# Keys of two token blocks by pairs of tiles, seven products in place of eight

## The chip, the cores and the metric

The kernel runs on one core of a Trainium2 chip. The metric is the device time of one execution in microseconds (us). All data are float32; TensorE gets every operand as two parts, a high part (the value rounded by a copy on ScalarE) and a low part (the rest, a subtraction on VectorE), and each product is three matmuls: high by high, high by low, low by high.

## The reference, cut to what matters

```python
# attention branch, S = 2048 tokens, D = 512, 32 heads of 16
q, k, v = split(x @ wqkv)
phi = lambda t: where(t > 0, t + 1, exp(t)) + 1e-6
kv  = einsum("bhsd,bhse->bhde", phi(k), v);  z = sum over tokens of phi(k)
o   = phi(q) kv / (phi(q) z + 1e-6);         a = o @ wo
# expert branch: 8 experts, softmax of x @ w_gate over all of them
b   = sum over e of gate_e * (silu(x @ w1[e]) @ w2[e])
out = g * a + (1 - g) * b,   g = sigmoid(x . gate_w)
```

The change is in one stage only, called keys: `phi(x @ wk)` for all tokens, ten more columns of the same product (eight gate logits, `x . gate_w` and a zero column), and y = sum over tokens of x^T phi(k), from which kv is made later.

## The kernel before, in words

The program has two stages, `keys` and `experts`, and every engine works through its instructions in the order in which the program issues them (the schedule is written by hand). The keys stage ends after some 96 us; the experts fill the rest. The 2048 tokens are four blocks of 512 (`tb` 0 to 3), each of four tiles of 128 tokens; the 512 features are four slices of 128 (`k`).

For one tile, `g_proj` (L482) makes two groups of the key columns, 256 and 266 wide (the second with the ten extra columns): for each of the four slices three matmuls (L454), 24 in all. `g_done` (L457) evicts a group: `phi_first` (L73) is an exponential and a relu on ScalarE (L74, L75), `phi_last` (L77) joins them on VectorE (L78). After the second group `eps_high` (L84, a ScalarE copy) and `eps_low` (L87, VectorE L88) make the high and low part `pkh` of the keys, VectorE copies the ten extra columns to `lg` (L470), and the keys are added to `pks`, their sum over tokens, by a DMA of GpSimd's queue that accumulates (L473 to L480; from the fifth tile on two tiles are added on VectorE first, L479). `split_xt` (L428) makes high and low part of the tile's tokens in row form, and `y_acc` (L489) adds x^T phi(k) into four PSUM banks `ys` with twelve matmuls 512 wide (L60 to L62). The loop over tiles (L558) issues both groups of tile t, then `split_xt(t)`, then `y_acc(t-1)`, then a list of further work (`beside`): splits of later token blocks (`split_x`), and what the experts need of the tokens.

The experts multiply in pairs of blocks with seven products in place of eight (Strassen-Winograd). For that the first stage makes sums of token blocks: `x_sum` (L498, four VectorE subtractions 1024 wide for each half of the tokens) and `x_part` (L504), which splits a sum into high and low part (one ScalarE copy and one VectorE subtraction, 1024 wide). The first half's seven operands stay in `XO[0]`; the second half's go to a DRAM room `xstash` (`x_keep`, and DMAs in `x_part`, L515) and come back later. `m.prep` (L190) prepares the first expert operands; `touch` (L649) opens the experts on TensorE.

PSUM has eight banks: two with tag "a", one "b", one "c", four "dn" (the four `ys`). Loads are issued on SyncE's queue: `load_x` (L381, a block of tokens by features, 1 MB), `load_xt` (L424, the block by rows, 1 MB). Tiles with one tag share a fixed number of rooms; a new tile waits until the last reader of the room's old one is through.

Of the kernel before, what the change touches and what calls it, by code (L numbers as in the profile page):

```python
# [16 lines left out]
P = 128  # L17
S = 2048
D = 512
# [304 lines left out]
def keys(m):  # L324
# [4 lines left out]

    banks_of = [0]  # L330
# [16 lines left out]
    def x_tiles(tb, K):  # L347
        if (tb, K) in ((0, 0), (0, 1), (1, 1)):
            X[tb, K] = [m.x_tile(f"x{tb}{K}{c}") for c in "hl"]
        elif (tb, K) == (3, 1):  # L350
            X[tb, K] = [m.x_tile(f"x{tb}{K}{c}", "xs") for c in "hl"]
        else:
            X[tb, K] = [att.tile([P, 2, TB], F32R, name=f"x{tb}{K}{c}", tag="xe", bufs=6) for c in "hl"]
# [18 lines left out]

    def room(name, dt=F32):
        return att.tile([P, 2048], dt, name=name, tag="raw", bufs=4)
# [11 lines left out]
    def split_x(tb, k):  # L386
        if k % 2 == 0:
            x_tiles(tb, k // 2)
        split(raw[tb][:, k, :], xk(0, tb, k), xk(1, tb, k))
# [5 lines left out]
    gw = [att.tile([P, 2 * KT * w], F32R, name=f"g{i}") for i, w in enumerate((256, 320))]  # L395
    gw = [g.rearrange("p (c k f) -> p c k f", c=2, k=KT)[:, :, :, :n] for g, n in zip(gw, G)]
    g0, g1 = gw
    x0 = raw[0] = four(room("x0"))
    r0 = four(m.raw_tile("r0")[:, :KT * G[0]])
    r1 = [hl_tile(f"r1{i}", F32) for i in range(2)]  # L400
# [4 lines left out]
    for k in range(KT):  # L405
        for lo, hi in pieces(k):
            nc.sync.dma_start(x0[:, k, lo:hi], m.xT[0][:, k * TB + lo:k * TB + hi])
        for w in ((0,), (1, 2), (3,), ())[k]:
            queue = nc.scalar if w < 2 else nc.sync
            queue.dma_start(r0[:, w, :], m.wk[:, w * G[0]:(w + 1) * G[0]])  # L410
    for i in range(2):
        at = KT * G[0] + 2 * i * G[1]
        nc.sync.dma_start(r1[i][:, :, :G[1]], m.wk[:, at:at + 2 * G[1]].rearrange("p (k f) -> p k f", k=2))
    x_tiles(0, 0), x_tiles(0, 1)
    for k in range(KT):
        for lo, hi in pieces(k):
            act_copy(xk(0, 0, k, lo, hi), x0[:, k, lo:hi])
        split(r0[:, k, :], g0[:, 0, k, :], g0[:, 1, k, :], v.tensor_copy if k == 0 else act_copy)
        v.tensor_sub(xk(1, 0, k), x0[:, k, :], f32(xk(0, 0, k)))
# [8 lines left out]
    def split_xt(t):  # L428
        if t < 12:
            xt[t] = m.w1p.tile([P, 2, TB], F32R, name=f"xt{t}", tag="o", bufs=4)  # L430
        else:
            xt[t] = att.tile([P, 2, TB], F32R, name=f"xt{t}", tag="xe", bufs=6)
# [12 lines left out]
    def bands(t):  # L445
        if t == 5:
            band(mask.rearrange("p (b e) -> p b e", e=DH), [[-DH, P // DH], [0, DH]], 1)

    pk, pk_last = {}, [None]
# [7 lines left out]
    def g_done(t, g, ps):  # L457
        if g == 0:
            if t < NTT:
                h = att.tile([P, 2, TB], F32R, name=f"pkh{t}", tag="xe", bufs=6)  # L460
            else:
                h = hl_tile(f"pkh{t}")
            pk[t] = pks_room if t == 0 else sf_tile(f"pk{t}"), h
            m.phi(pk[t][0][:, :G[0]], ps)
        else:
            d, h = pk[t]
            m.phi(d[:, G[0]:], ps[:, :D - G[0]])
            m.eps_high(h[:, 0], d)
            m.eps_low(h[:, 1], d, h[:, 0])
            v.tensor_copy(lg[:, t, :E + 2], ps[:, D - G[0]:])  # L470

            if t == 0:
                nc.gpsimd.dma_start(pks, d)  # L473
            elif t < NTT:
                nc.gpsimd.dma_start(pks, d, accum_op=ALU.add)
            elif t % 2 == 0:
                pk_last[0] = d
            else:
                v.tensor_add(d, d, pk_last[0])  # L479
# [24 lines left out]
    def x_part(p, i):  # L504
# [16 lines left out]

    idle = dn_bank("idle")
    for i in range(7):
        nc.tensor.matmul(idle, zero[:, :P], zero, start=True, stop=True)
    banks = [up_bank(f"g0_{t}")[:, :G[0]] for t in range(NTT)]
    for k in range(KT):
        for j in range(3):
            for t in range(NTT):
                g_pass(t, 0, k, j, banks[t])
    load_xt(0)  # L530
    load_x(1)
    for k in range(KT):
        split(r1[k // 2][:, k % 2, :G[1]], g1[:, 0, k, :], g1[:, 1, k, :])
    for t in range(NTT):
        g_done(t, 0, banks[t])
    for t in range(NTT):
        split_xt(t)
        g_proj(t, 1, dn_bank if t < 2 else up_bank)
    ys = [dn_bank(f"y{i}") for i in range(KT)]
    load_xt(1)  # L540
    load_x(2)
# [776 lines left out]
```

## Time and profile before

| | us |
|---|---|
| median of 3 runs (2317.18 to 2318.82) | 2317.56 |
| the profiled execution | 2317.11 |
| its span in the profile | 2315.4 |
| TensorE busy | 2309.3 |
| VectorE busy | 1829.0 |
| ScalarE busy | 1407.1 |
| keys: first matmul of the last `y_acc` | 92.85 |
| experts: first matmul (`touch`) | 95.59 |

The span is taken from the first to the last record; the execution's own time lies 1.7 us above it. A row of the timeline gives start, duration, engine, line, operation, output and input. Durations of matmuls are modelled and overlap: the distance from one start to the next is what a matmul costs on TensorE. On ScalarE and VectorE the next queued operation starts some 0.1 us before the recorded end of the one ahead of it.

### The profile page before, as it was taken

The numbers are of one execution on the slowest core, as the hardware profiler recorded it, in microseconds if no ns is written. First come the engines' busy times: TensorE is split into PE (matmuls) and PEld (weight loads), VectorE is DVE, ScalarE is ACT, GpSimd is POOL, SyncE is SP. The second block draws the span as 40 slices with busy tenths as digits, with TensorE's granted clock in tenths as the row PEclk, the third lists the DMA queues.
The fourth block names the chain that finished last, engine by engine and source line by source line (L and its number), as shares of the span: only waits on it lengthen the run. The fifth ranks groups of instructions, "written<-read, shape, count | busy, mean of one in ns | idle before, by whom it ended". The sixth has DMA issues, their size and how long they took to land.

```text
span 2315.4 us, 31620 instructions
## 1 busy us (share of the span) xinstructions
PE 2309.3 (100%) x10546; PEld 1917.3 (83%) x10546; DVE 1829.0 (79%) x3136; ACT 1407.1 (61%) x2654; POOL 156.8 (7%) x216
## 2 busy tenths in 40 slices
PE   9999999999999999999999999999999999999999
PEld 8888888888888888888888888888888888888887
DVE  7899888888888888888677768776677777877777
ACT  6687666666666666666555556555565655655553
POOL 1101000000000000000001000000011101000001
PEclk9999999999999999999999999999999999999999
DMA  6799888988889898888856455664556746566568
GB/s 224 222 306 294 269 277 257 286 258 266 268 270 280 253 293 254 264 269 259 297 146 168 151 179 151 185 186 137 161 175 183 189 147 182 164 164 175 162 219 226
DMA packets 323044, 510.29 MB, mean 220 GB/s; under 512 B 52080, under 2 KB 220416, under 8 KB 322496
## 3 DMA queue, kind: packets, MB, share of 16 engines
q1 hardware_dynamic: 294256, 462.53, 61.2%
q0 software_dynamic: 22912, 44.68, 11.2%
q10 hardware_dynamic: 5712, 1.05, 0.2%
q8 instruction: 83, 1.36, 0.2%
q14 instruction: 81, 0.66, 0.1%
HBM read 342.41 MB, written 163.13 MB: 218 GB/s over the span
## 4 chain that ended last, share of the span: by engine, by line
PE 100%; DVE 0%; issue 0%
PE p L60 16%; PE p L62 16%; PE p L61 16%; PE a L60 9%; PE a L61 9%; PE a L62 9%; PE c L60 5%; PE c L62 5%; PE c L61 5%; PE b L60 2%; PE b L62 2%; PE b L61 2%; PE g L454 2%; PE y L60 1%; PE y L62 1%; PE y L61 1%
## 5 line engine op out<-in xcount | busy, mean ns | idle before, releaser
L62 PE MATMUL p<-ho,w 128*128 128x512 f32 x1602 | 623.3, 389 | 0.0
L60 PE MATMUL p<-ho,w 128*128 128x512 f32 x1602 | 623.2, 389 | 0.0
L61 PE MATMUL p<-ho,w 128*128 128x512 f32 x1602 | 623.2, 389 | 0.0
L790 DVE TENSOR_TENSOR ho<-s,ho 128x512 fp32r<-128x512 f32 x784 | 536.2, 685 | 38.9 <-ACT ho L65 36.3
L65 ACT ACTIVATE ho<-s 128x512 fp32r<-128x512 f32 x784 | 481.5, 621 | 17.4 <-PE p L62 11.0
L60 PEld LDWEIGHTS p<-ho,w 128*128 128x128 f32 x1602 | 300.8, 188 | 62.5
L61 PEld LDWEIGHTS p<-ho,w 128*128 128x128 f32 x1602 | 300.8, 188 | 62.3
L62 PEld LDWEIGHTS p<-ho,w 128*128 128x128 f32 x1602 | 300.6, 188 | 62.4
L65 ACT ACTIVATE o<-rs 128x512 fp32r<-128x512 f32 x224 | 129.1, 576 | 203.6 <-PE c L62 114.1
L65 ACT ACTIVATE o<-rm 128x512 fp32r<-128x512 f32 x240 | 138.4, 577 | 142.4 <-PE a L62 65.6
L716 DVE TENSOR_TENSOR s<-c,s 128x512 f32<-128x512 f32 x116 | 80.1, 691 | 156.2 <-PE c L62 148.0
L65 ACT ACTIVATE ws<-rm 128x256 fp32r<-128x256 f32 (+1 forms) x204 | 114.6, 571 | 46.0 <-DMA w2stash<-ws 40.5
L628 ACT ACTIVATE s<-s 128x512 f32<-128x512 f32 x224 | 138.4, 618 | 6.1 <-DVE s L721 3.5
L628 ACT ACTIVATE s<-b 128x512 f32<-128x512 f32 x112 | 67.0, 599 | 103.1 <-PE b L62 98.1
L65 ACT ACTIVATE s<-a 128x512 f32<-128x512 f32 x116 | 69.1, 595 | 91.2 <-PE a L62 91.2
L205 DVE TENSOR_TENSOR o<-rm,o 128x512 fp32r<-128x512 f32 x180 | 123.0, 683 | 1.3 <-ACT o L65 1.2
L721 DVE TENSOR_TENSOR s<-a,s 128x512 f32<-128x512 f32 x116 | 79.7, 687 | 52.1 <-PE a L62 52.0
L205 DVE TENSOR_TENSOR o<-rs,o 128x512 fp32r<-128x512 f32 x168 | 114.1, 679 | 5.1 <-ACT o L65 5.1
L219 DVE TENSOR_TENSOR ws<-rm,ws 128x512 fp32r<-128x512 f32 x155 | 106.1, 684 | 14.3 <-ACT ws L65 12.6
L65 ACT ACTIVATE b<-a 128x512 f32<-128x512 f32 x116 | 67.2, 579 | 61.1 <-PE a L62 61.1
L849 POOL DMA_DIRECT2D acct<-c x30 | 25.8, 869 | 914.6 <-DVE c L843 712.8
L65 ACT ACTIVATE s<-c 128x512 f32<-128x512 f32 x116 | 68.9, 594 | 22.3 <-PE c L62 22.3
(317 smaller groups left out, 4529.8 us busy)
## 6 DMA issues: line engine op xcount, KB each, us to landing
w<-w2stash SPq DMA_DIRECT2D x403, 512.0 KB, 4.1
w2stash<-ws SPq DMA_DIRECT2D x359, 256.0 KB, 4.6
rm<-wm SPq DMA_DIRECT2D x228, 256.0 KB, 5.2
rs<-wm SPq DMA_DIRECT2D x108, 256.0 KB, 4.0
wb<-wgtd SPq DMA_DIRECT2D x16, 512.0 KB, 4.8
acct<-c POOLq DMA_DIRECT2D x30, 256.0 KB, 6.0
acct<-d POOLq DMA_DIRECT2D x30, 256.0 KB, 5.4
acct<-k POOLq DMA_DIRECT2D x30, 256.0 KB, 5.3
```

Source lines behind the costliest of these rows:

```text
L60: nc.tensor.matmul(ps, wh, xh, start=start, stop=False, skip_group_check=True)
L61: nc.tensor.matmul(ps, wh, xl, start=False, stop=False, skip_group_check=True)
L62: nc.tensor.matmul(ps, wlo, xh, start=False, stop=stop, skip_group_check=True)
L65: nc.scalar.activation(dst, src, AF.Copy, scale=scale, bias=bias)
L205: v.tensor_sub(two(o, 1), src, f32(two(o, 0)))
L219: v.tensor_sub(two(w, 1), src, f32(two(w, 0)))
L454: nc.tensor.matmul(ps, xk((0, 0, 1)[j], tb, k, tt * P, (tt + 1) * P), gw[g][:, (0, 1, 0)[j], k, :], start=(k == 0 and j == 0), stop=(k == ...
L628: nc.scalar.activation(dst, src, AF.Silu)
L716: v.tensor_add(sn[g, 2], bank[g, "c"], sn[g, 2])
L721: v.tensor_add(sn[g, 3], bank[g, "a"], sn[g, 3])
L790: v.tensor_sub(h[1], s, f32(h[0]))
L849: nc.gpsimd.dma_start(m.acct[part.h, j, dt], s, accum_op=ALU.add)
```

## The change

The blocks are taken in the order 2, 3, 0, 1 (`ORD`). Blocks 2 and 3 are done tile by tile as before; the group of 266 columns comes first now, the ten extra columns are copied on ScalarE, and none of these eight tiles is added to another on VectorE. For blocks 0 and 1 the tiles j of both blocks are a pair: the two tiles' keys are a 2 by 2 product (two tiles by two halves of the features, two halves of the features by two halves of the key columns), and seven products of six matmuls each make it (`product`, 266 wide for four of them, 256 for three), with the token sums `XO[0]` that the experts use anyway as the stationary operand, and sums of wk's four blocks as the moving one. These sums are new: `w_load` reads a part of wk a second time, `w_sums` makes four sums on VectorE, and `w_part` splits four of them. The seven products run in banks a, b and c, with a copy of bank a to b and two evictions to `s2` and `s3` on ScalarE, and two additions on VectorE, for each pair. `group`, `late` and `flush` put phi and its splits into the queues; `extra` holds the further work of each pair. `y_acc` can be issued in halves. The token sums of the first half must be ready before the pairs, so those of the second half are made during the pairs, and the raw blocks 2 and 3 are loaded a second time for them (`load_x(2)`, `load_x(3)`); the second half's four split sums share one room (`raw["t"]`) from which they are stored. `m.prep(0, 1)` to `(0, 7)` are issued between the last two `y_acc`.

```diff
+    ORD = (2, 3, 0, 1)
+    ND = 2 * NTT
+    W = (G[1], G[0])
+    OFF = (KT * G[0], 0)
+    WS = (320, 256)
...
+        if (tb, K) == (3, 0):
             X[tb, K] = [att.tile([P, 2, TB], F32R, name=f"x{tb}{K}{c}", tag="xe", bufs=6) for c in "hl"]
+        else:
+            X[tb, K] = [m.x_tile(f"x{tb}{K}{c}", "xs" if tb == 3 else "x") for c in "hl"]
...
-        return att.tile([P, 2048], dt, name=name, tag="raw", bufs=4)
+        return att.tile([P, 2048], dt, name=name, tag="raw", bufs=3)
...
+    sums_of = []
+    def pk_tile(t, h):
+        pk[t] = sf_tile(f"pk{t}") if t != ORD[0] * NTT else pks_room, h
+        return pk[t]
+    def pk_done(t, alone):
+        d, h = pk[t]
+        m.eps_high(h[:, 0], d)
+        m.eps_low(h[:, 1], d, h[:, 0])
+        if alone:
+            sums_of.append(t)
+            nc.gpsimd.dma_start(pks, d, **({} if len(sums_of) == 1 else {"accum_op": ALU.add}))
+        elif not m.odd:
+            m.odd = [d]
+        else:
+            v.tensor_add(d, d, m.odd.pop())
+            nc.gpsimd.dma_start(pks, d, accum_op=ALU.add)
+    m.odd = []
+    def group_done(t, g, src):
+        d = pk[t][0]
+        if g == 0:
+            act_copy(lg[:, t, :E + 2], src[:, HALF:W[0]])
+        m.phi(d[:, HALF:] if g == 0 else d[:, :HALF], src[:, :HALF])
     def g_pass(t, g, k, j, ps):
@@ -454,44 +491,29 @@
         nc.tensor.matmul(ps, xk((0, 0, 1)[j], tb, k, tt * P, (tt + 1) * P), gw[g][:, (0, 1, 0)[j], k, :],
                          start=(k == 0 and j == 0), stop=(k == KT - 1 and j == 2))
-    def g_done(t, g, ps):
+    def g_done(t, g, ps, alone):
         if g == 0:
-            if t < NTT:
-                h = att.tile([P, 2, TB], F32R, name=f"pkh{t}", tag="xe", bufs=6)
-            else:
-                h = hl_tile(f"pkh{t}")
-            pk[t] = pks_room if t == 0 else sf_tile(f"pk{t}"), h
-            m.phi(pk[t][0][:, :G[0]], ps)
-        else:
-            d, h = pk[t]
-            m.phi(d[:, G[0]:], ps[:, :D - G[0]])
-            m.eps_high(h[:, 0], d)
-            m.eps_low(h[:, 1], d, h[:, 0])
-            v.tensor_copy(lg[:, t, :E + 2], ps[:, D - G[0]:])
-            if t == 0:
-                nc.gpsimd.dma_start(pks, d)
-            elif t < NTT:
-                nc.gpsimd.dma_start(pks, d, accum_op=ALU.add)
-            elif t % 2 == 0:
-                pk_last[0] = d
-            else:
-                v.tensor_add(d, d, pk_last[0])
-                nc.gpsimd.dma_start(pks, d, accum_op=ALU.add)
-    def g_proj(t, g, bank=up_bank):
-        ps = bank(f"g{g}_{t}")[:, :G[g]]
+            pk_tile(t, xe_tile(f"pkh{t}"))
+        group_done(t, g, ps)
+        if g:
+            pk_done(t, alone)
...
-        g_done(t, g, ps)
-    def y_acc(t):
-        _, ph = pk.pop(t)
-        xh = xt.pop(t)
-        for c in range(KT):
+        g_done(t, g, ps, alone)
+    ycount = []
+    def y_acc(t, part=None):
+        ph, xh = pk[t][1], xt[t]
+        if part != 1:
+            ycount.append(t)
+        for c in range(KT) if part is None else (2 * part, 2 * part + 1):
             cs = slice(c * P, (c + 1) * P)
-            mm3(ys[c], xh[:, 0, cs], xh[:, 1, cs], ph[:, 0], ph[:, 1], t == 0, t == NT - 1)
...
             h, lo = XO[0][i] = [m.x_tile(f"t{i}{c}") for c in "hl"]
         else:
-            both = room(f"t{i}", F32R).rearrange("p (c k f) -> p c k f", c=2, k=2)
-            h, lo = both[:, 0], both[:, 1]
+            if "t" not in raw:
+                raw["t"] = room("t", F32R).rearrange("p (c k f) -> p c k f", c=2, k=2)
+            h, lo = raw["t"][:, 0], raw["t"][:, 1]
         split(r, h, lo)
         if p:
...
+    def oh_tile(name):
+        return f32(m.w1p.tile([P, 2, HALF], F32R, name=name, tag="oh", bufs=2)).rearrange("p c f -> p (c f)")
+    w0 = [oh_tile(f"w0{i}").rearrange("p (k f) -> p k f", k=2) for i in range(2)]
+    (w00, w01), (w10, w11) = w0, r1
+    def w_load():
+        src = m.wk[:, OFF[0]:OFF[0] + KT * W[0]].rearrange("p (k f) -> p k f", k=KT)
+        for i in range(2):
+            nc.sync.dma_start(w0[i], src[:, 2 * i:2 * i + 2, :HALF])
+    def w_sums():
+        v.tensor_add(w11, w10, w11)
+        v.tensor_sub(w10, w00, w10)
+        v.tensor_sub(w00, w11, w00)
+        v.tensor_sub(w01, w01, w00)
+    def w_part(i):
+        src = {1: w11, 5: w10, 3: w00, 4: w01}[i]
+        if i in wide:
+            o = wide[i]
+            act_copy(o[:, :, :, HALF:], f32(gw[0][:, :, :2, HALF:] if i == 1 else gw[0][:, :, 2:, HALF:]))
+        else:
+            o = m.w1p.tile([P, 2, D], F32R, name=f"wsum{i}", tag="ws", bufs=2).rearrange("p c (k f) -> p c k f", k=2)
+        split(src, o[:, 0, :, :HALF], o[:, 1, :, :HALF])
+        KO[i] = o
+    KO = {0: gw[0][:, :, :2], 2: gw[0][:, :, 2:], 6: gw[1][:, :, 2:]}
...
+    load_xt(ORD[1])
+    load_x(ORD[2])
+    w_load()
     for t in range(NTT - 1):
-        y_acc(t)
-        split_x(1, t)
-    split_x(1, KT - 1)
-    beside = {t: [] for t in range(NTT, NT)}
-    for k in range(KT):
-        beside[4 + k // 2].append(lambda k=k: split_x(2, k))
-        beside[8 + k // 2].append(lambda k=k: split_x(3, k))
-        beside[(4, 5, 6, 6)[k]].append(lambda k=k: x_sum(0, k))
-        beside[(7, 7, 8, 9)[k]].append(lambda k=k: x_part(0, (1, 5, 3, 6)[k]))
-        beside[(10, 10, 12, 12)[k]].append(lambda k=k: x_sum(1, k))
-        beside[(11, 11, 13, 13)[k]].append(lambda k=k: x_part(1, (1, 5, 3, 6)[k]))
-        beside[14].append(lambda k=k: m.prep(0, k))
-        beside[15].append(lambda k=k: m.prep(0, 4 + k))
-    rows_of = {12: (12, 13), 13: (14, 15), 14: (), 15: ()}
-    for t in range(NTT, NT):
-        if t in (4, 8):
-            load_xt(t // 4 + 1)
-        if t == 5:
-            load_x(3)
-        if t in (12, 14):
-            m.load(t // 2 - 6)
-        bands(t)
+        y_acc(T0 + t)
+        split_x(ORD[1], t)
+    split_x(ORD[1], KT - 1)
+    load_x(ORD[3])
+    x_keep(0, (2, 0)), x_keep(2, (2, 1))
+    A, B = ORD[2], ORD[3]
+    beside = {
+        0: (lambda: w_sums(), lambda: w_part(1), lambda: split_x(A, 0)),
+        1: (lambda: split_x(A, 1), lambda: split_x(A, 2), lambda: split_x(A, 3), lambda: w_part(4)),
+        2: (lambda: x_sum(0, 0), lambda: split_x(B, 2), lambda: split_x(B, 3), lambda: x_part(0, 1)),
+        3: (lambda: x_sum(0, 1), lambda: x_sum(0, 2), lambda: x_part(0, 3)),
+    }
+    T1 = ORD[1] * NTT
+    for t in range(NTT):
         for g in range(2):
-            g_proj(t, g)
-        for row in rows_of.get(t, (t,)):
-            split_xt(row)
-        y_acc(t - 1)
+            g_proj(T1 + t, g, alone=True)
+        split_xt(T1 + t)
+        y_acc(T1 + t - 1)
         for do in beside[t]:
             do()
-        if t in (6, 9, 10):
-            i, key = {6: (0, (2, 0)), 9: (2, (2, 1)), 10: (4, (3, 1))}[t]
-            x_keep(i, key)
-    y_acc(NT - 1)
+        if t == 1:
+            x_keep(4, (3, 1))
+            load_xt(A)
+            band(mask.rearrange("p (b e) -> p b e", e=DH), [[-DH, P // DH], [0, DH]], 1)
+    XO[0][0], XO[0][2], XO[0][4] = X[A, 0], X[A, 1], X[B, 1]
+    load_xt(B)
+    load_x(2)
+    bank, sn = {}, {}
+    def product(j, i, b, start):
+        xh, xl = XO[0][i]
+        o = KO[i]
+        n = W[0] if i in (0, 1, 2, 4) else HALF
+        ts = slice(j * P, (j + 1) * P)
+        for k in range(2):
+            mm3(b[:, :n], xh[:, k, ts], xl[:, k, ts], o[:, 0, k, :n], o[:, 1, k, :n], start and k == 0, k == 1)
+    def touch():
+        nc.tensor.matmul(m.ps_tile("kb", "b")[:, :W[0]], XO[0][0][0][:, 0, :P], KO[0][:, 0, 0, :W[0]], start=True,
+                         stop=True)
+    late = []
+    def flush():
+        while late:
+            late.pop(0)()
+    def group(t, g, src, done):
+        d = pk[t][0]
+        if g == 0:
+            act_copy(lg[:, t, :E + 2], src[:, HALF:W[0]])
+        dst, src = d[:, HALF:] if g == 0 else d[:, :HALF], src[:, :HALF]
+        m.phi_first(dst, src)
+        late.append(lambda: m.phi_last(dst, src))
+        if done:
+            late.append(lambda: pk_done(t, False))
+    def pair(j, extra):
+        top, bot = A * NTT + j, B * NTT + j
+        a = m.ps_tile(f"ka{j}", "a")
+        product(j, 0, a, True)
+        flush()
+        b = m.ps_tile(f"kb{j}", "b")
+        act_copy(b[:, :W[0]], a[:, :W[0]])
+        yield
+        c = m.ps_tile(f"kc{j}", "c")
+        product(j, 1, c, True)
+        s3 = oh_tile(f"k3_{j}")[:, :HALF]
+        act_copy(s3, c[:, :HALF])
+        yield
+        product(j, 2, b, False)
+        extra(0)
+        pk_tile(top, hl_tile(f"pkh{top}"))
+        group(top, 0, b, False)
+        yield
+        product(j, 3, a, False)
+        s2 = oh_tile(f"k2_{j}")[:, :W[0]]
+        act_copy(s2, a[:, :W[0]])
+        flush()
+        extra(1)
+        yield
+        product(j, 4, c, False)
+        extra(2)
+        v.tensor_add(s2, c[:, :W[0]], s2)
+        pk_tile(bot, xe_tile(f"pkh{bot}"))
+        group(bot, 0, s2, False)
+        yield
+        product(j, 5, a, False)
+        flush()
+        extra(3)
+        v.tensor_add(s3, a[:, :HALF], s3)
+        group(bot, 1, s3, True)
+        yield
+        product(j, 6, a, False)
+        flush()
+        group(top, 1, a, True)
+    def last_step(run):
+        for _ in run:
+            pass
+    more = {
+        0: ((lambda: w_part(3),), (lambda: w_part(5), lambda: x_part(0, 5)),
+            (lambda: split_xt(4), lambda: x_sum(0, 3)), (lambda: x_part(0, 6), lambda: split_xt(0), lambda: load_x(3))),
+        1: ((), (lambda: split_xt(5),), (lambda: x_sum(1, 0), lambda: x_part(1, 1)),
+            (lambda: split_xt(1), lambda: x_sum(1, 1))),
+        2: ((lambda: split_xt(6, True),), (lambda: x_part(1, 5), lambda: split_xt(2, True)),
+            (lambda: x_sum(1, 2), lambda: split_xt(7, True)),
+            (lambda: split_xt(3, True), lambda: m.load(0), lambda: m.load(1))),
+        3: ((lambda: x_part(1, 3),), (lambda: x_sum(1, 3),), (lambda: x_part(1, 6),), (lambda: m.prep(0, 0),)),
+    }
+    old = None
+    touch()
+    for j in range(NTT):
+        before = (B * NTT + j - 1, A * NTT + j - 1) if j else (T1 + NTT - 1, None)
+        def extra(i):
+            for do in more[j][i]:
+                do()
+        run = pair(j, extra)
+        for _ in range(3):
+            next(run)
+        if old:
+            last_step(old)
+        y_acc(before[0], 0)
+        next(run)
+        y_acc(before[0], 1)
+        next(run)
+        if j and j < NTT - 1:
+            y_acc(before[1], 0)
+        next(run)
+        if j:
+            y_acc(before[1], 1 if j < NTT - 1 else None)
+        old = run
+    last_step(old)
+    flush()
+    y_acc(B * NTT + NTT - 1)
+    for k in range(1, 8):
+        m.prep(0, k)
+    y_acc(A * NTT + NTT - 1)
     m.ys = ys
```

More of the change, by code (lines that the diff above doesn't have):

```diff
@@ L392, in keys @@
     v.memset(f32(zero), 0.0)
[L395 to L400, printed above, removed]
+    gw = [att.tile([P, 2 * KT * w], F32R, name=f"g{i}").rearrange("p (c k f) -> p c k f", c=2, k=KT)[:, :, :, :n]
+          for i, (w, n) in enumerate(zip(WS, W))]
+    wide = {i: att.tile([P, 2 * 2 * 272], F32R, name=f"wide{i}").rearrange("p (c k f) -> p c k f", c=2, k=2)[:, :, :, :W[0]]
+            for i in (1, 4)}
+    tb0 = ORD[0]
+    x0 = raw[tb0] = four(room(f"x{tb0}"))
+    r0 = m.raw_tile("r0")[:, :KT * W[0]].rearrange("p (k f) -> p k f", k=KT)
+    r1 = [hl_tile(f"r1{i}", F32)[:, 0].rearrange("p (k f) -> p k f", k=2) for i in range(2)]
     def pieces(k):
```

61 lines of the change are left out of this document (27 added, 34 removed).

## The prediction

> **What bounds the kernel now.** I read the page first, then the chain that ended last, then TensorE's, ScalarE's and VectorE's timelines of the keys stage, since all of the change lies there.
>
> ```profile
> span 2315.4 us, 31620 instructions
> PE 100%; DVE 0%; issue 0%
> ```
> ```profile
> 25.49 2.91 PE g L454 x24
> ...
> 87.38 2.91 PE g L454 x24
> 93.70 0.23 PE y L60
> ```
> ```profile
> 92.85 0.39 PE L60 MATMUL y<-pkh,xt 128*128 128x512 f32 x1
> ...
> 95.59 0.39 PE L652 MATMUL b<-x00h,o 128*128 128x512 f32 x1
> ```
>
> TensorE is the chain from end to end. In the keys stage a tile's two groups cost 2.91 us (24 matmuls of 0.121) and a `y_acc` 95.59 - 92.85 = 2.74 (12 of 0.228; 1.37 for half of one). No matmul waits. So a matmul less is time won, and any wait that a new order gives TensorE is time lost: nothing later catches it up. How much room do the two evicting engines have?
>
> ```profile
> core 0: us, PE busy (x) PEld busy (x) DVE busy (x) ACT busy (x) POOL busy (x), PEclk, DMA share, GB/s
> 42.20:47.80 5.60, 5.60 (x37) 5.16 (x36) 4.75 (x9) 2.75 (x8) 0.00 (x0) 1.00 0.26 47
> 47.80:53.50 5.70, 5.70 (x38) 5.19 (x37) 5.00 (x11) 4.38 (x9) 0.86 (x1) 1.00 0.42 98
> ```
> ```profile
> DVE pkh L88 <- ACT pkh L65: 11.2, 16, 0.7
> ACT pkh L65 <- DVE pk L78: 9.8, 16, 1.2
> DVE pk L78 <- ACT g L75: 5.0, 9, 1.5
> ```
>
> VectorE is busy 4.75 to 5.00 us of each tile's 5.6, and most of what is left is the waits in the second fence: phi and its split are a chain that passes between ScalarE and VectorE. It hides because `y_acc(t-1)` follows the groups of tile t: a whole tile of matmuls lies between an eviction and its use. One tile's eviction, TensorE's first row after its groups, then ScalarE, then VectorE:
>
> ```profile
> 45.12 0.39 PE L60 MATMUL y<-pkh,xt 128*128 128x512 f32 x1
> ```
> ```profile
> 45.31 0.39 ACT L74 ACTIVATE pk<-g 128x256 f32<-128x256 f32 x1 [0.76 <-PE g L454]
> 45.59 0.38 ACT L75 ACTIVATE g<-g 128x256 f32<-128x256 f32 x1
> 46.46 0.63 ACT L65 ACTIVATE pkh<-pk 128x512 fp32r<-128x512 f32 x1 [0.49 <-DVE pk L78]
> 47.00 0.62 ACT L65 ACTIVATE xt<-xr 128x512 fp32r<-128x512 f32 x1
> 47.52 1.04 ACT L65 ACTIVATE t1h<-x 128x1024 fp32r<-128x1024 f32 x1
> ```
> ```profile
> 45.48 0.94 DVE L78 SCALAR_TENSOR_TENSOR pk<-pk,g 128x256 f32<-128x256 f32 x2
> 47.12 0.69 DVE L88 SCALAR_TENSOR_TENSOR pkh<-pk,pkh 128x512 fp32r<-128x512 f32 x1 [0.70 <-ACT pkh L65]
> 47.73 0.16 DVE L470 COPY lg<-g 128x10 f32<-128x10 f32 x1
> 47.85 0.69 DVE L479 TENSOR_TENSOR pk<-pk,pk 128x512 f32<-128x512 f32 x1
> 48.46 0.68 DVE L342 TENSOR_TENSOR xt<-xr,xt 128x512 fp32r<-128x512 f32 x1
> 49.06 1.22 DVE L342 TENSOR_TENSOR t1l<-x,t1h 128x1024 fp32r<-128x1024 f32 x1
> ```
> ```profile
> L502 DVE TENSOR_TENSOR x<-x,x 128x1024 f32<-128x1024 f32 x6 | 7.3, 1220 | 0.1
> L78 DVE SCALAR_TENSOR_TENSOR pk<-pk,g 128x256 f32<-128x256 f32 x32 | 12.8, 416 | 5.1 <-ACT g L75 5.0
> L65 ACT ACTIVATE b<-a 128x512 f32<-128x512 f32 x116 | 67.2, 579 | 61.1 <-PE a L62 61.1
> ```
>
> From these rows the prices in a queue, start to start: ScalarE 0.28 at 256 wide, 0.53 at 512, 0.95 at 1024; VectorE 0.35, 0.60, 1.15 to 1.24. Where the next step is on the other engine the whole duration counts: 0.4, 0.65, 1.05 and 0.42, 0.69, 1.22. ScalarE starts 0.2 after TensorE is through (45.31 against 45.12).
>
> **The change part by part.**
>
> *Matmuls.* A pair had 48 (5.82 us) and gets 42 (5.09; 0.74 a product of 266, 0.72 one of 256). Four pairs: -2.9; the new `touch` adds 0.12. So -2.8 us; everything else is a question of waits.
>
> *Order and first eight tiles.* The groups only change places. Four copies to `lg` go to ScalarE (the trace has no such copy from PSUM; between L470's 0.16 and L74's 0.39; I take 0.1 in the queue, 0.2 alone) ahead of the first `y_acc`.
>
> ```profile
> 15.81 0.69 DVE L88 SCALAR_TENSOR_TENSOR pkh<-pk,pkh 128x512 fp32r<-128x512 f32 x1 [0.69 <-ACT pkh L65]
> ...
> 17.17 0.39 PE L60 MATMUL y<-pkh,xt 128*128 128x512 f32 x1
> ```
>
> Its slack is 17.17 - 16.50 = 0.67, the copies take 0.4 to 0.8 of it: 0 to 0.2, taken as 0. SyncE's queue gets 2.5 MB more (raw blocks 2 and 3 again, part of wk), and two stores to `xstash` come some 20 us earlier. What is loaded early is used 15 us later or more, twice the landing times below; it costs nothing, and the two that are late stand under the bounds.
>
> ```profile
> xr<-x SPq DMA_DIRECT2D x4, 1024.0 KB, 7.4
> xstash<-t SPq DMA_DIRECT2D x8, 512.0 KB, 4.1
> x<-xT SPq DMA_DIRECT2D x3, 1024.0 KB, 9.1
> ```
>
> *Into the pairs.* Beside the tiles of block 3 VectorE gets four sums of wk (0.7 each, by L479), two `w_part`, six `split_x`, three `x_sum`, two `x_part`: 13.6 us on top of 4 x 2.0 for the tiles' own work, in 22.5 us less the waits. Laid one after another, the lists of the first three tiles end at 35.5, 40.6 and 46.8, so the last tile's phi starts at 46.8 (45.9 without backlog), and then, in queue order: two phi 47.55, `eps_high` 48.2, `eps_low` 48.85, row split 49.45, two `x_sum` 51.9, ScalarE's copy in `x_part(0, 3)` 52.9. Behind that copy on ScalarE's queue stands pair 0's copy of bank a to b (0.4, between 0.38 and 0.58): 53.3. Product 2 accumulates on b. TensorE comes to it at 45.1 + 2.74 + 0.12 + 2 x 0.74 = 49.5, and all matmuls stand behind it. **Wait 3.9** (3.0 without backlog).
>
> *From pair to pair.* `flush` at the next pair's product 0 puts phi, `eps_high` and `eps_low` of the lower tile ahead of the copy to b. So product 2 of the next pair ends a chain that begins with this pair's product 3. After the end of pair 1's product 3, in program order, each step at its end: copy to s2 0.5; `eps_high` of the old upper tile 1.1; `eps_low` 1.8; sum of the pair's keys 2.5; split of rows 3.1; `x_sum` 4.3; copy of `x_part(1, 1)` 5.4, its low part 6.5; only now the addition to s2, which stands behind `extra(2)`, 7.0; copy to `lg`, exponential, relu 7.8; phi 8.2; split of rows 8.9; `x_sum` 10.1; addition to s3 10.5; exponential, relu 11.1; phi 11.6; `eps_high` 12.25; copy to b 12.6; matmul 12.7. TensorE's own work between is two and then one half `y_acc` (3 x 1.37) and products 4, 5, 0, 1 (2.9): 7.0. **Wait 5.7.**
>
> Pair 0 by the same laying out: s2, copies of `w_part(5)` and `x_part(0, 5)` 2.0, low part 3.2, rows 3.8, `x_sum` 5.0, add 5.4, relu 6.2, `x_part(0, 6)` 8.3, rows 8.9, add 9.3, then as above 11.5; TensorE has only one half `y_acc` and four products, 4.3. **Wait 7.2.** Pair 2: `x_part(1, 5)` to 3.7, rows 4.2, `x_sum` 5.4, rows 6.0, add 6.4, phi 7.6, rows 8.4, add 8.8, copy to b 10.9: 11.0 against 7.0. **Wait 4.0.** Pair 3, up to its lower tile's `y_acc`: `x_sum` 3.7, `x_part(1, 6)` 6.0, add 6.4, phi 7.6, add 8.0, phi 9.1, `eps_low` 10.5: 10.6 against 1.37 + 0.74 + 0.72 + 2.74 + 0.72 = 6.3. **Wait 4.3.**
>
> *Into the experts.* `prep(0, 1)` to `(0, 7)` are 4 us of VectorE behind the last sum of keys and end about 0.8 after `touch`, where they are needed 1.5 later; 0 to 1, taken as 0.
>
> **Sum.** 3.9 + 7.2 + 5.7 + 4.0 + 4.3 = 25.1 of waits, less 2.8: +22.3. The profiled execution's own time is 2317.11 (0.45 under the median), so **2339.4**.
>
> Bounds: the trace shows none of these waits. By the shorter price at every step and no backlog they come to about 20 (2334). Upward, pair 1's `x_sum` needs block 3's second load, issued when `x_part(0, 6)` is through, some 9 us before; at 9.1 it lands just in time, and a load 2.5 late adds as much. `x_part(1, 6)` overwrites a room whose store (4.1) began some 5 before. With durations of the upper row ends the waits come to 30 (2344).
>
> **The rivals.**
>
> *The clock falls in the waits.*
>
> ```profile
> PEclk9999999999999999999999999999999999999999
> ```
> ```profile
> 1.52 3.36 PE L524 MATMUL idle<-zero 128*128 128x512 f32 x7 [1.52 <-DVE zero L392]
> 4.89 1.44 PE L454 MATMUL g<-g,x00h 128*128 128x256 f32 x8
> ```
>
> The first seven matmuls, after no work, cost 0.48 each where the same shape costs 0.228 later. If each of the four waits over 3 us (3.9, some 5.2 of pair 0's, 4.8, 3.7) is followed by such 3.36 us, each loses 3.36 - 7 x 0.228 = 1.8, and fully, because products 2 and 3 lie on the chain: +7, **2346**. Against: the page's clock row shows no fall, but TensorE never idled there. [...]
>
> *Half of it.* Only the backlog (entry and pair 0) stalls, because VectorE and ScalarE catch up in the longer waits and the later chains overlap better than laid out: -2.8 + 11.1 = +8.3, **2325**. Against: pairs 1 and 2 give VectorE 8 to 9 us of work of 10.6, with some 3 us of engine-to-engine waits on top.
>
> *Not slower.* The turn from product 3 to the next product 2 fits TensorE's 7.0 us; then only the matmuls count, 2317.1 - 2.8 = **2314.3**. It decides at that one point: the copy to b must start by 6.5 after product 3. For it: VectorE's work on average (21.6 beside block 3, 17.2 the pairs' own, 19.2 their further work, 4.0 `prep`: 62 us of 70) still fits. Against: 12.7 laid out; it would need the chain cut to half.
>
> **How the numbers follow.** Forecast 2339.4 (its own range 2333 to 2344): 0.52. Clock 0.2; half of it 0.14; not slower 0.12; 0.02 for something else. A measurement of this kernel can tell about 0.2%, 4.6 us, from no change; 2314.3 is within it, so same 0.12, faster 0.02 (only TensorE's 2.8 us are to be had), slower 0.86. The range leaves out "not slower" and the end of the clock's case: 2321 to 2349.
>
> **What would show it.** The profile after should have TensorE idle before the first matmuls of product 2 into b, released by ScalarE's copy from a, in four groups of 3.7 to 5.3 us between 48 and 100 us, and near the end of the keys before product 6 and a `y_acc`; `touch` of the experts near 118 in place of 95.6; the experts as long as before. Matmul work of the keys should be 2.8 us less. Wrong would be the forecast if the copies to b start as soon as product 0 ends, or if VectorE has done `x_sum` and `x_part` before product 4 ends; the clock's rival shows in start-to-start distances near 0.24 at 256 wide.

## The result and the profile after

The changed kernel takes **2351.89 us** (2350.45 to 2353.25, four runs) against 2317.37 of the kernel before (2317.04 to 2318.82): a ratio of 1.0148, 95% interval 1.0130 to 1.0165. That is 34.5 us slower, 12.5 over the forecast and 3 over the upper end of its range. The profiled execution took 2351.11.

From the page of the kernel after, span, busy time of TensorE, its clock row and the chain that ended last:

```profile
span 2349.4 us, 31599 instructions
...
PE 2320.7 (99%) x10523; PEld 1924.3 (82%) x10523; DVE 1835.6 (78%) x3132; ACT 1416.9 (60%) x2686; POOL 158.0 (7%) x218
...
PEclk9899999999999999999999999999999999999999
...
PE 95%; ACT 0%; DVE 0%; issue 0%
```

and the same busy row of the kernel before:

```profile
PE 2309.3 (100%) x10546; PEld 1917.3 (83%) x10546; DVE 1829.0 (79%) x3136; ACT 1407.1 (61%) x2654; POOL 156.8 (7%) x216
```

10546 - 24 + 1 = 10523: the four pairs have lost their 24 matmuls and `touch` is one more. Yet TensorE is busy 11.4 us *longer*, and the chain that ended last, TensorE alone before, is now followed back only to 118.05 us, where it runs over ScalarE and VectorE. Busy time that grows while work shrinks means slower matmuls, and the clock row has an 8 in its second slice (58.7 to 117.5 us), which lies in the keys stage. The experts start late and then run as before: their first matmul, `touch`, stands at 130.22 in place of 95.59 (34.6 later), the spans differ by 34.0.

What TensorE waited for in the first 130 us of the kernel after (us in total, times, longest):

```profile
PE kb L60 <- ACT kb L65: 17.8, 4, 5.4
PE ka L60 <- DVE k L696: 2.5, 1, 2.5
...
PE kc L60 <- DVE k L689: 1.2, 2, 0.6
PE y L60 <- ACT pkh L65: 0.9, 1, 0.9
PE ka L62 <- DVE t5l L352: 0.8, 1, 0.8
```

The top line is four waits for ScalarE's copy into bank b. They and two waits near the end (2.5 and 0.9) stand at the places that the forecast named. TensorE's timeline at the first of them:

```profile
53.57 0.59 PE L60 MATMUL kb<-g,x01h 128*128 128x266 f32 x1 [3.54 <-ACT kb L65]
...
55.06 0.63 PE L60 MATMUL y<-pkh,xt 128*128 128x512 f32 x1
55.49 0.63 PE L61 MATMUL y<-pkh,xt 128*128 128x512 f32 x1
...
58.91 0.50 PE L60 MATMUL y<-pkh,xt 128*128 128x512 f32 x1
59.24 0.40 PE L61 MATMUL y<-pkh,xt 128*128 128x512 f32 x1
59.48 0.40 PE L62 MATMUL y<-pkh,xt 128*128 128x512 f32 x1
```

Behind the wait a 512-wide matmul takes 0.43 from start to start (55.49 - 55.06), later 0.24 (59.48 - 59.24). The row at 58.91 took 0.33, between the two, so the rate changed inside it, at 59.13. In stretches of time (TensorE busy, its weight loads, VectorE, ScalarE, GpSimd, then the granted clock):

```profile
53.50:58.90 5.40, 5.33 (x18) 4.75 (x19) 2.02 (x3) 1.56 (x6) 0.00 (x0) 0.50 1.00 315
...
70.80:76.20 5.40, 5.35 (x19) 4.78 (x20) 1.28 (x3) 1.69 (x6) 0.00 (x0) 0.50 0.00 0
76.20:82.00 5.80, 5.80 (x35) 5.17 (x34) 3.12 (x4) 2.19 (x4) 0.85 (x1) 1.00 0.16 28
```

The clock is at exactly a half in the stretches behind the waits, with the DMA engines fully busy (1.00) in the one and idle in the other. Read in this way there are five such stretches: 53.57 to 59.13, 70.85 to 76.21, 89.99 to 93.30, 106.92 to 110.34 and 121.89 to 127.42, together 23.2 us. With 0.43 in place of 0.23 that is 46% lost: 10.7 us. The granted clock as the trace records it agrees: it is a half from 52.30 to 59.13, 69.37 to 76.20, 86.44 to 93.26, 106.92 to 110.33 and 120.57 to 127.40. Four of these five begin while TensorE still waits, or between the two last waits; the one at 106.92 begins 0.5 after its wait.

**The sum at `touch`.** The entry is pair 0's product 2; a turn is the stretch from one pair's product 3 to the next pair's product 2. Waits from start to start: 3.7 at the entry; 0.9 + 0.8 + 5.6 in pair 0's turn; 0.7 + 5.2 in pair 1's; 4.0; at the end 2.7 + 1.2; together 24.8 (the view's 23.2, and some 0.18 at each because the matmuls on both sides of a wait are further apart). Clock 10.7; the two matmuls behind the last wait 0.5 more; the first tiles 0.4; matmuls -2.8. That is 33.6 of 34.6; one microsecond I could not place.

### The profile page after: what moved, and what is told of

Same layout as the page of the kernel before. It is cut to its first block, busy times and chain, and to the rows that moved or that the text cites. A ratio compares the mean times of both kernels' runs of the same rounds, so it can differ in the third digit from the quotient of the medians.

```text
span 2349.4 us, 31599 instructions
## 1 busy us (share of the span) xinstructions
PE 2320.7 (99%) x10523; PEld 1924.3 (82%) x10523; DVE 1835.6 (78%) x3132; ACT 1416.9 (60%) x2686; POOL 158.0 (7%) x218
## 4 chain that ended last, share of the span: by engine, by line
PE 95%; ACT 0%; DVE 0%; issue 0%
PE p L60 15%; PE p L62 15%; PE p L61 15%; PE a L60 9%; PE a L62 9%; PE a L61 9%; PE c L60 4%; PE c L62 4%; PE c L61 4%; PE b L62 2%; PE b L61 2%; PE b L60 2%; PE s L60 0%; PE s L62 0%; PE s L61 0%; PE y L60 0%
```

## The experiments

The theory after the result: two losses that add up, (a) waits of TensorE behind chains through ScalarE's and VectorE's in-order queues, some 25 us; (b) a clock that falls because TensorE stood still, some 11. Rivals: the slow stretches come from something else in the change (its operands, what the other engines read and write meanwhile), and the waits come from the two engines having too much to do, whatever the order.

### Fillers, with late zeros

Matmuls by zeros, called fillers here, go into TensorE's queue ahead of the places where it waits. They add nothing to `y`.

```diff
+    zz = att.tile([P, P], F32R, name="zz")
+    nc.gpsimd.memset(f32(zz), 0.0)
+    def warm(n):
+        for _ in range(n):
+            nc.tensor.matmul(ys[0][:, :HALF], zz, gw[1][:, 0, 0, :], start=False, stop=False, skip_group_check=True)
...
+        warm(26 if j != 1 else 36)
         product(j, 2, b, False)
...
+        if j == NTT - 1:
+            warm(20)
         product(j, 6, a, False)
+        if j == NTT - 1:
+            warm(6)
```

> The kernel after, with matmuls by a stationary operand of zeros (256 wide, 0.12 us each, adding nothing to y) put into TensorE's queue ahead of product 2 (26, 36, 26, 26 of them), ahead of pair 3's product 6 (20) and behind it (6). They fit into the waits that the trace shows (3.7, 5.6, 5.2, 4.0, 2.7, 1.2 us). Theory (queue waits of 24.9 us, and some 11 us more because the clock falls in those waits): product 2 starts where it did relative to the product 3 before it, the distances behind the waits go back from 0.22 and 0.43 to 0.12 and 0.23, and the time falls by 10 to 12 us, to about 2341. Rival (the matmuls behind the waits are slow for another cause, reads of the same memory by the other engines or by DMAs): the distances stay 0.22 and 0.43 and the time stays at 2350 to 2353, or rises by what the fillers cost.

2356.57 us, ratio 1.0168 (1.0153 to 1.0183). The timeline tells why it says nothing yet:

```profile
61.33 5.92 PE L651 MATMUL y<-g,zz 128*128 128x256 f32 x26 [11.72 <-POOL zz L647]
```

The memset of the zeros was queued on GpSimd behind the DMAs that it issues (it ran at 60.74), and the first filler waited 11.7 us for it. An operation that looks free has the place in its queue that program order gives it.

### Fillers, with early zeros

The same, but VectorE writes the zeros at the very start:

```diff
     v.memset(f32(zero), 0.0)
+    zz = att.tile([P, P], F32R, name="zz")
+    v.memset(f32(zz), 0.0)
```

> As e1_warm, with the zeros written by VectorE at the very start, so that no filler waits for them. Theory (the clock falls after each wait of some 3 us or more and costs five stretches, 11.2 us in the trace of after): the same waits of some 25 us until the bank b is ready, filled with zero matmuls, but no stretch of 256-wide matmuls at 0.22, so 2340 to 2343 us. Rival (the slow stretches have another cause, such as the memory that VectorE and ScalarE share, and the waits alone make the time): 2350 to 2354. Second rival (the fillers are themselves too long and delay product 2): above 2354, with product 2 released by TensorE itself and not by ScalarE's copy.

**2342.70 us** (2342.19 to 2345.05), ratio 1.0108 (1.0091 to 1.0125). From the last real matmul to product 2 it is still 3.7, 5.6, 5.2 and 4.0 us: the waits are the same, only filled. What changed is the rate behind them, and that is worth 9.2 us. One stretch stayed slow, and it is telling. TensorE's waits, and the place on its timeline:

```profile
PE kb L60 <- ACT kb L65: 4.2, 4, 1.9
```
```profile
85.37 0.39 PE L60 MATMUL kb<-g,x01h 128*128 128x266 f32 x1 [1.89 <-ACT kb L65]
85.60 0.28 PE L61 MATMUL kb<-g,x01h 128*128 128x266 f32 x1
...
86.08 0.41 PE L62 MATMUL kb<-g,x01l 128*128 128x266 f32 x1
86.30 0.41 PE L60 MATMUL ka<-g,t6h 128*128 128x256 f32 x1
```

There the fillers ended 1.9 us too early. The matmuls resume at full rate (85.60 to 85.84 in steps of 0.12) and fall to half at 86.08, *after* the wait was over, until 89.52. So the rate is not a matter of which matmuls run, and 1.9 us can be enough.

### Gaps in the kernel before

To see the clock without the change: the kernel before, with a pause ahead of the groups of each of tiles 4 to 15. It multiplies zeros and adds them to `y`.

```diff
...
+    STEPS = (3, 5, 7, 9, 4, 6, 8, 10, 2, 5, 7, 6)
+    def probe(n):
+        for i in range(2):
+            nc.tensor.matmul(ys[0][:, :P], zz, gap, start=False, stop=False, skip_group_check=True)
+            for _ in range(n if i == 0 else 0):
+                nc.gpsimd.memset(f32(gap), 0.0)
...
+        probe(STEPS[t - NTT])
```

> The kernel before, with one idle gap of TensorE ahead of the groups of each of tiles 4 to 15: two zero matmuls of 128 columns with 2 to 10 small GpSimd memsets between them, so gaps of about 1.5 to 6 us. Theory (the granted clock falls when TensorE stands still for about 2.5 to 4 us, and stays at half for 3 to 5.5 us after the end of the wait whatever is multiplied): gaps under 2.5 us are followed by 0.12 per 256-wide matmul, gaps of 4 us and more by 0.22 to 0.24 for 3 to 5.5 us, a loss of 1.6 to 2.9 us each; in sum some 45 us of gaps and 8 to 15 us of slow stretches. Rival (the slow stretches of after come from its own matmuls and operands, not from standing still): no gap is followed by slow matmuls.

2374.73 us, ratio 1.0247 (1.0227 to 1.0268). There are twelve pauses of 0.8 to 3.7 us (and one of 11.5 ahead of them, in which the first matmul waited for its zeros), and slow matmuls behind some of them, in a kernel without the change's operands: the first rival is out. The theory took the length of a pause to decide, and it does not. Pauses of 2.48, 2.68 and 3.52 were followed by half rate at once; one of 3.73 only 1.4 us after its end; and one of 3.47 not at all (the first two steps behind it are 0.14, then 0.12; rows marked x2 hold two matmuls):

```profile
134.69 0.33 PE L566 MATMUL y<-gap,zz 128*128 128x128 f32 x1 [3.47 <-POOL gap L568]
134.86 0.45 PE L454 MATMUL g<-g,x30h 128*128 128x256 f32 x2
135.14 0.28 PE L454 MATMUL g<-g,x30l 128*128 128x256 f32 x1
```

The slow stretches end at 44.42, 61.49, 71.71, 81.96, 102.46 and 112.68, and these are 5, 3, 3, 6 and 3 times 3.41 us apart, each within 0.07. In the kernel after they end at 59.13, 76.21, 93.30, 110.34 and 127.42, each 5 times 3.41 apart. So the clock is set at the borders of windows of 3.41 us that run on their own: in the recorded clock of the kernel before and of the kernel after every change lies on a grid of 3.413 us, within 0.01 over the whole execution (677 and 687 windows from the first change to the last).

### The same gap twelve times

This gave a sharper forecast: of equal pauses some must cost and some not.

```diff
+    STEPS = (8, 8, 8, 8, 8, 8, 8, 8, 8, 8, 8, 8)
```

> As e5_probe, with the same 8 memsets in each of the twelve gaps, so about 2.2 us of idle TensorE each, some longer where GpSimd's queue is held. Theory (the clock is set by windows of 3.41 us that run freely; one in which TensorE idles for over some 1.85 us is followed by one at half rate, and full rate comes back after a window idle for under some 0.4): of gaps with the same length some cost 1.7 us and some nothing, by where they lie to the windows; of 2.2 us gaps about half; the ends of the slow stretches are multiples of 3.41 us apart. Rival (the length of the gap alone decides): all gaps of 2.2 us cost alike, or none does, and a slow stretch starts with the end of its gap.

2387.62 us, ratio 1.0302 (1.0282 to 1.0323). Six pauses came out at 2.22 us each; four were followed by half rate and two were not. One of each kind on TensorE's timeline (the second pause follows below the dots):

```profile
71.79 0.33 PE L566 MATMUL y<-gap,zz 128*128 128x128 f32 x1 [2.22 <-POOL gap L568]
71.95 0.56 PE L454 MATMUL g<-g,x10h 128*128 128x256 f32 x2
72.31 0.41 PE L454 MATMUL g<-g,x10l 128*128 128x256 f32 x1
...
94.14 0.33 PE L566 MATMUL y<-gap,zz 128*128 128x128 f32 x1 [2.22 <-POOL gap L568]
94.30 0.45 PE L454 MATMUL g<-g,x20h 128*128 128x256 f32 x2
94.59 0.28 PE L454 MATMUL g<-g,x20l 128*128 128x256 f32 x1
```

This run's borders lie at 68.73, 72.14 and 92.62. Busy time and granted clock of three of its windows:

```profile
68.73:72.14 3.41, 1.19 (x8) 0.86 (x7) 3.38 (x5) 0.40 (x1) 1.64 (x8) 1.00 0.00 0
72.14:75.55 3.41, 3.41 (x17) 3.41 (x17) 0.39 (x2) 0.66 (x2) 0.00 (x0) 0.50 0.00 0
...
92.62:96.03 3.41, 1.89 (x15) 1.90 (x16) 1.86 (x3) 0.64 (x2) 1.18 (x6) 1.00 0.02 5
```

The first pause, 69.57 to 71.79, lies in one window, and the clock falls at 72.14; the second, 91.92 to 94.14, is cut by a border into 0.70 and 1.52. Counted over the windows of the eleven traces that have pauses, no window that idled under 1.5 us was followed by half rate, every one that idled over 2.0 was, and between the two both occur (1.52, 1.78 and 1.89 yes, 1.74 and 1.92 no). A slow window that idled under 0.2 us was followed by full rate every time, one that idled over 0.5 by another slow one every time.

### The order within a pair

The copy to b goes ahead of `flush`, and two lists of further work go behind the addition and the first part of phi:

```diff
         product(j, 0, a, True)
-        flush()
         b = m.ps_tile(f"kb{j}", "b")
         act_copy(b[:, :W[0]], a[:, :W[0]])
+        flush()
...
-        extra(2)
         v.tensor_add(s2, c[:, :W[0]], s2)
         pk_tile(bot, xe_tile(f"pkh{bot}"))
         group(bot, 0, s2, False)
+        extra(2)
...
-        extra(3)
         v.tensor_add(s3, a[:, :HALF], s3)
         group(bot, 1, s3, True)
+        extra(3)
```

> The kernel after with the same instructions in another order: in a pair the copy of bank a to b is issued ahead of the flush, and the further work that stood ahead of the two additions (the third and fourth list of a pair) behind them and behind the exponential and relu that follow. Theory (the next product 2 waits for the in-order queues of VectorE and ScalarE): the turns from product 3 to the next product 2 go from 11.5, 12.7, 11.0 us to about 8.9, 9.5, 9.0, the waits in all from 24.9 to about 17.5, with one or two fewer stretches at the low clock: about 2340 (2336 to 2344). Rival (the waits lie in the data path itself, product to copy to product, or in loads): unchanged, 2350 to 2353.

2343.02 us (2341.68 to 2343.95), ratio 1.0110 (1.0095 to 1.0125). TensorE's waits:

```profile
PE kb L60 <- ACT kb L65: 12.5, 4, 4.8
PE ka L60 <- DVE k L695: 2.2, 1, 2.2
...
PE y L60 <- ACT pkh L65: 1.9, 2, 1.0
PE ka L62 <- DVE t5l L352: 0.8, 1, 0.8
```

17.4 in place of 23.2: nothing was removed, only the order changed, and 8.9 us came back, 5.8 of it waits and the rest clock. Of four waits for b two are now 2.1 us long, and one of these still cost a slow window.

### Half of the further work

The token sums of the second half (blocks 2 and 3) and their splits are left out; the first half's operands are stored in their place, so that the transfers stay.

```diff
-        v.tensor_sub(dst, x, y)
+        if p == 0:
+            v.tensor_sub(dst, x, y)
...
+        if p:
+            for c in range(2):
+                nc.sync.dma_start(m.xstash[i, c], f32(XO[0][i][c]).rearrange("p k t -> p (k t)"))
+            return
```

> Leaves out the token sums of the second half and their splits (4.8 us of VectorE and 4 us of ScalarE in pairs 1 to 3); the first half's operands are stored in their place, so the second half of the tokens comes out of other numbers, with all matmuls, loads and stores as in the kernel after. Theory: entry 3.7 and pair 0 (0.9 + 0.8 + 5.6) wait as before, the later turns come down to 7.8, 8.5 and pair 3 to about 7 against 7.0, 7.0 and 6.3 of TensorE's own work, so 25 us of waits become 14, and the low clock is left behind two waits instead of five: 2333 to 2337. Rival (seven products in three banks need this time whatever the queues hold): at least 2348.

2336.35 us (2335.80 to 2337.76), ratio 1.0082 (1.0067 to 1.0097). Waits at b 12.0 in place of 17.8; the 5.4 of pair 0's turn, which this doesn't touch, is still the longest. VectorE is busy 9.8 us less (1825.8 in place of 1835.6): the expectation's 4.8 are the sums alone, without the low parts. The further work is in the chains of pairs 1 to 3, as laid out, and is not the whole of them.

### The sums on GpSimd

```diff
-        v.tensor_sub(dst, x, y)
+        nc.gpsimd.tensor_sub(dst, x, y)
```

> The kernel after with all eight token-block subtractions (1024 wide) on GpSimd instead of VectorE. Theory: VectorE's queue loses 1.2 us each; the entry wait shrinks by what two of them cost less what GpSimd takes longer, and pair 1's turn loses the 1.2 us of the subtraction that stands ahead of the second addition. If GpSimd takes about 1.2 us for one: waits 4 to 6 us less, 2343 to 2349. If it takes 2.4 us or more, or if its queue holds them behind the accumulating DMAs that wait for VectorE: no gain, 2350 to 2358. Rival (VectorE's load is not the cause): unchanged within 1 us with GpSimd as fast as VectorE.

2366.96 us, ratio 1.0215 (1.0198 to 1.0232): worse by 15, and 9 over the upper end of what was expected. Groups of this kernel between 44 and 135 us and of the kernel after between 44 and 130, the mean of one instruction in ns behind the busy time:

```profile
L524 POOL TENSOR_TENSOR x<-x,x 128x1024 f32<-128x1024 f32 x6 | 16.1, 2677 | 0.2
```
```profile
L524 DVE TENSOR_TENSOR x<-x,x 128x1024 f32<-128x1024 f32 x6 | 7.3, 1221 | 0.0
```

A subtraction takes 2.68 us on GpSimd against 1.22 on VectorE. GpSimd's, VectorE's and ScalarE's timelines of this kernel, and one of TensorE's waits:

```profile
50.17 0.87 POOL L472 DMA_DIRECT2D pks<-pk  x1 [1.85 <-DMA pks<-pk]
50.77 2.66 POOL L524 TENSOR_TENSOR x<-x,x 128x1024 f32<-128x1024 f32 x1
```
```profile
57.13 3.44 DVE L88 SCALAR_TENSOR_TENSOR pkh<-pk,pkh 128x512 fp32r<-128x512 f32 x1 [0.70 <-ACT pkh L65]
60.49 2.82 DVE L352 TENSOR_TENSOR xt<-xr,xt 128x512 fp32r<-128x512 f32 x1
```
```profile
53.46 1.06 ACT L65 ACTIVATE t1h<-x 128x1024 fp32r<-128x1024 f32 x1 [9.75 <-POOL x L524]
```
```profile
PE kb L642 <- DVE pk L78: 8.2, 1, 8.2
```

Two things went wrong. The first subtraction stood in GpSimd's queue behind the DMAs that add keys to `pks` and started at 50.77, where VectorE had started it at 43.52 in the kernel after. ScalarE stood idle 9.75 us for it and the last tile's phi came late behind it on both engines, so TensorE waited 8.2 us ahead of pair 0, at a place where the kernel after doesn't wait. And five VectorE instructions that met a running subtraction took 2.38 to 3.44 us (the two rows above among them), where others of the same lines took 0.69 at 512 wide and 1.23 at 1024: 9.9 us more, about what taking the eight subtractions away had freed (8 of 1.22). By what a subtraction holds VectorE up no run here shows. How the 15 us divide between the two was not tested.

### Rearranged, and rearranged with fillers

The order above; the split `w_part(3)` of one of wk's sums ahead of the entry; the whole `y_acc` of block 3's last tile ahead of pair 0's product 2; each tile's keys added to `pks` by a DMA of their own; the lists of further work spread anew:

```diff
-            late.append(lambda: pk_done(t, False))
+            late.append(lambda: pk_done(t, True))
...
-        3: (lambda: x_sum(0, 1), lambda: x_sum(0, 2), lambda: x_part(0, 3)),
+        3: (lambda: x_sum(0, 1), lambda: x_sum(0, 2), lambda: w_part(3), lambda: x_part(0, 3)),
...
+        if j == 0:
+            y_acc(before[0])
```

> The change with its further work rearranged: the copy of a to b ahead of flush, each extra list behind the additions and the phi of its product, wk's third sum ahead of the entry, the upper half's y_acc whole ahead of pair 0's product 2, and each tile's keys added to pks by their own DMA and not first on VectorE. Theory (the waits are chains of in-order queues: shorter chains, shorter waits, and fewer waits long enough for the clock): waits of about 10 us in place of 25, one or two slow stretches (2 to 4 us), 2328 to 2333. Rival (the two engines' sum of work sets the waits, whatever the order): as e2_order, 2341 to 2345.

2336.80 us (2336.68 to 2336.95), ratio 1.0083 (1.0068 to 1.0098): between the two expectations, some 4 over the upper end of the theory's. TensorE's waits:

```profile
PE kb L60 <- ACT kb L65: 8.7, 4, 4.6
PE y L60 <- ACT pkh L65: 1.9, 2, 1.0
...
PE ka L60 <- DVE k L695: 1.5, 1, 1.5
PE kc L60 <- DVE k L688: 1.2, 1, 1.2
```

13.3 where I had looked for 10, of which pair 0's turn has 4.6. With fillers added (4, 22, 12 and 10 ahead of product 2, 14 ahead of the last product 6):

> e6_combo with zero matmuls of VectorE's early zeros ahead of each product 2 (4, 22, 12, 10) and ahead of the last pair's product 6 (14). Theory: e6_combo's waits, without its slow stretches, 2 to 5 us under e6_combo. Rival: no slow stretch is left in e6_combo, and the fillers give nothing or cost up to 2 us.

**2333.64 us** (2332.38 to 2334.45), ratio 1.0069 (1.0054 to 1.0084), 3.2 under the same kernel without them: the clock again, apart from the waits. Without fillers four windows are slow (two from 62.15, two from 106.52), with them one, behind a wait of 1.93. It is the best form of the change here and still 16 us slower than the kernel before; with no wait at all only the 2.8 us of matmuls would be won.

### Without the copy

```diff
-        act_copy(b[:, :W[0]], a[:, :W[0]])
...
-        product(j, 2, b, False)
+        product(j, 2, b, True)
```

> The change without the copy of bank a to b: product 2 starts bank b afresh, so the upper tiles' first group lacks product 0, and all else is as it was. Theory (ScalarE's copy, queued behind the phi of the tile before, is the lock; the two engines' work would fit): no wait at kb is left (17.8 in after), the waits at kc and ka grow to 6 to 9 us in all, one or two windows at half rate, 2326 to 2334 us. Rival (VectorE and ScalarE need the time anyway, and TensorE only meets them at the next bank): waits of 18 us and more, now at kc and ka, 2342 to 2350.

2343.33 us (2342.61 to 2343.72), ratio 1.0110 (1.0093 to 1.0127). TensorE's waits:

```profile
PE ka L60 <- DVE k L695: 7.3, 4, 2.5
PE y L60 <- ACT pkh L65: 4.1, 4, 1.0
PE ka L60 <- ACT wsum L65: 1.9, 1, 1.9
```

The time is the rival's, the waits are between the two. Those at b are gone, as they must be; but with the smaller ones 14.4 us stand at the next banks, two pauses of 2.0 to 2.5 and 1.0 in most turns, and these cost five slow stretches again (two windows each in two of them). So the copy decides where TensorE meets the two engines, and some 9 of 23 us of idle time; the rest stays without it, at the two engines' next results.

## Why the forecast missed

**Matmuls, -2.8**: right; 24 fewer and `touch`, by count, and 0.73 a product.

**The waits, 25.1**: right in place, cause and size, though all were laid out from durations of a kernel that had none. Entry 3.9, measured 3.7; pair 0's turn 7.2, measured 7.3 (part of it at t5l and c, on the way to b); pair 1's 5.7, measured 5.9; pair 2's 4.0, measured 4.0; the end 4.3, measured 3.9. The chain at the entry, on ScalarE's timeline of the kernel after:

```profile
52.18 1.06 ACT L65 ACTIVATE t3h<-x 128x1024 fp32r<-128x1024 f32 x1 [3.23 <-DVE x L524]
53.14 0.38 ACT L65 ACTIVATE kb<-ka 128x266 f32<-128x266 f32 x1
```

ScalarE stood idle 3.23 us in front of a copy that waited for VectorE's second `x_sum`, with the copy to b behind it; the forecast had this copy end at 52.9 and the one to b at 53.3, they ended at 53.2 and 53.5. Pair 1's turn came out step by step too, on VectorE and then on ScalarE:

```profile
82.34 1.23 DVE L352 TENSOR_TENSOR t<-x,t 128x1024 fp32r<-128x1024 f32 x1 [1.13 <-ACT t L65]
```
```profile
89.56 0.37 ACT L65 ACTIVATE kb<-ka 128x266 f32<-128x266 f32 x1
```

From the end of product 3 (76.91) the `x_sum` ended after 4.3 (laid out: 4.3), the low part of `x_part(1, 1)` after 6.7 (6.5), the addition to s3 after 10.7 (10.5) and the copy to b after 13.0 (12.6). That `prep` and the experts' first operands cost nothing held as well. So neither "Half of it" nor "Not slower" came about: pairs 1 and 2 waited too.

**The clock**: this is the step that failed. The forecast took the clock to hold through the waits, on the page's row of nines. That row could not speak for it: before the change TensorE never idled in this stage. The rival "The clock falls in the waits" had the mechanism, and its time, 2346, was too low for two reasons. It counted four waits over 3 us, and there were five slow stretches: the wait at the end, 2.5 + 0.9 after being split, was enough as well. And it gave each a fixed 3.36 us, as at the start, 1.8 of loss; the windows of 3.41 made it 5.6, 5.4, 3.3, 3.4 and 5.5 us. The 3.54 us at the entry fell into two windows (2.27 us of idle time in the one, 1.27 in the next): the first made the second slow, and the second, slow and again partly idle, made the third slow. So 10.7 in place of 7, and in place of the forecast's 0.

That each wait over 3 us, and no shorter one, is followed by a slow stretch was the author's estimate in that rival; the rows of before, where TensorE never idles in this stage, show no such limit. What the runs showed in its place: 1.89 us were enough with early zeros, 3.47 cost nothing among the gaps, and the ends of the slow stretches lie multiples of 3.41 apart; the idle time in a window decides, and not the length of the wait.

What the runs show of causes: that the slow stretches come from standing still (pauses alone make them in the kernel before, fillers take them away in the kernel after); that the order in the two queues sets a good part of the waits. How short the waits could be made by another arrangement stays open; the best one tried left 13 us.

## What to carry to other kernels

When a change makes a saturated TensorE wait, price the wait twice: its length, and one or two windows of 3.41 us at half rate (1.6 or 2.6 us here) as soon as about half a window is idle (here between 1.5 and 2.0 us of the 3.41). A saving in matmuls that puts their results on a chain through two in-order queues has to pay for the whole chain: here 2.8 us of matmuls bought 25 of waits. Where a wait can't be avoided, multiplying zeros through it buys the clock back (9.2 us here), if the zeros themselves are early (the late ones held TensorE up for 11.7).

## What the runs showed of the hardware

- In the traces of before and after the granted clock changed only at borders 3.413 us apart, each fitting within 0.01 us over 677 and 687 windows. Counted from the start of the span one lies at 59.13 in the kernel after, 61.49 with the gaps and 72.14 with equal gaps; these are no multiples of 3.413 apart. In the eleven traces with pauses the clock fell after every window with over 2.0 us of idle TensorE and after none with under 1.5, stayed at a half after slow windows that idled over 0.5, and was back after those that idled under 0.2.
- With early matmuls by zeros in the waits one of five slow stretches was left: the mean granted clock of the profiled execution was 0.999 in place of 0.993, the time 9.2 us less.
- A 128x1024 float32 subtraction took 2.68 us on GpSimd and 1.22 on VectorE; 512-wide VectorE instructions of two lines (`eps_low` and the row split) that met one on GpSimd took 2.82 to 3.44, others of the same lines 0.69.
